# A Mamba-2 scan with a SiLU feed-forward block: products inside the chunks ordered by halves of the heads, two groups of zero products fewer, another sequence in the ramp

## The chip, the cores and the metric

The kernel runs on one core of one Trainium2 chip. The core has TensorE (PE in the profile; its weight loads are shown apart as PEld), VectorE (DVE), ScalarE (ACT), GpSimd (POOL) and SyncE (SP), which here only issues transfers. The metric is device time in microseconds, the median of several executions.

## What is computed

Two stages. The first is a state-space scan for 4 batches, 8 heads, 768 positions, head size 32 and state size 16. Cut to one chunk of positions:

```python
cum = np.cumsum(log_a, axis=-1)
L = np.exp(cum[:, :, :, None] - cum[:, :, None, :]) * causal
M = np.einsum('bhin,bhjn->bhij', Cc, Bc) * L
y_intra = np.einsum('bhij,bhjd->bhid', M, xc)
y_inter = np.einsum('bhin,bhnd->bhid', Cc, state) * np.exp(cum)[:, :, :, None]
y = y_intra + y_inter
state = decay_full[:, :, None, None] * state + sum_j(B_j x_j * decay_from_j)
```

The second takes y as 3072 tokens of 256 values: `h = y @ w_in` (256 x 2048), `g = h / (1 + exp(-h))` (SiLU), `out = g @ w_out` (2048 x 256). All inputs and outputs are float32.

## The kernel before, in words

**Units.** The 3072 positions are cut into 12 units of 256 positions; u = 0 to 11, three to a batch. A unit holds four chunks of 64 positions (chunk t = 2k + c). Two units make a pair G of 512 tokens for the feed-forward block.

**The order is written out by hand.** `SCHEDULE` (line 18) is a long text of tokens such as `M,0,1`. The table `DO` (line 857) maps a token's name to a function, the numbers are its arguments, and the loop at line 870 calls them one after the other. Each function issues a few instructions; each engine runs its own instructions strictly in the order in which the tokens come, and waits on semaphores where an operand is not ready. So the text fixes five sequences, one for each engine, and the place of two tokens of different engines relative to one another means nothing by itself. `SLOTS` (line 98) says which buffer each new tile gets, in the order in which tiles are taken.

**The tokens that matter here**, with the line that the profile shows:

- Loads: `Ln` (B or C by rows, L245), `Lt` (B or C for a transpose, L253), `Lx` (x, L260), `lw` (a block of weights, L279), `ir` (the decays for all units, L357). SP issues nearly all of them; ACT issues the first of B and C.
- `z,n` and `z,0,6` (PE, L422 and L424): products on a tile of zeros whose result nobody reads. `z,1` is one product of 128x512, `z,0,6` is six products of 64x64.
- `ab` (PE, L478) spreads the decays over partitions, `E` (DVE, L487) scans them; the result, in the tile `ab`, is the decay matrix L transposed.
- `T` (DVE, L500) or `tp`/`tq` (PE L506, ACT L515) transpose B and C; `ce` (ACT, L521) masks C by parity of the head; `C` (POOL or DVE, L526) makes cw, which is C times the decay from the chunk's start.
- `P01` (DVE, L457): prefix products of the decays, fed by `PA` (POOL, L447) and `pb` (PE, L452).
- `B` (POOL, L495) and `D` or `gd` (PE, L548): B times decay, then its products with x, the new part of the state. `S,u,t` (DVE, L590 or L592): the state after chunk t. `SM` (ACT, L600): the state masked by parity.
- `g0` (PE, L562): the products of B and C, into the PSUM tiles ga (heads 0 to 3) and gb (heads 4 to 7), each two banks. `M,u,w` (DVE, L577): half w of the heads (0: heads 0 to 3 out of ga, 1: heads 4 to 7 out of gb) times the decay matrix, written in place into `ab`.
- `Y` (PE): `products` (line 603): first 32 products inside the chunks (L613, 64 rows by 32 columns, eight at a time beside each other on the array), M times x, into ga and gb; then the products of cw and the state (L622), added to them. `X0` (ACT, L652, units 0 and 1) or `y` (ACT, L658) copy y out.
- Feed-forward, pair 0: `s` (PE, L682), `si` (ACT, SiLU, L688), `n` (PE, L748), in plain float32. The other pairs split each float32 operand into parts of fewer bits (`xh`, `x`, `h`, `l`, `e`, and for the weights `u`, `v`, `w`, `W`, `H`, `Wl`, `Wd`, `We`) and use faster products: `a`, `d` (PE, L789) and `f` (PE, L770). `u`, `v` are ACT, `w` DVE, `W` POOL (L312); `s,u,j` needs `W,j`.
- `cI` makes the identity matrix `ident`: a memset on DVE (L368), then a select on POOL (L369). `co`, `AA`, `AD` (POOL) prepare the decays of the later units and store them to DRAM.

**The ramp.** Until the first feed-forward weights are prepared and y of unit 0 exists, PE has only small work: `ab`, `pb`, `tp`, `D`, `g0`, `Y` and zero products. Then `s,0,2` is the first product of the feed-forward block, and after `Y,1` the tokens `s,0,1 s,1,2 s,1,0 ...` follow one another. From there until the end, units 2 to 11 of the scan are woven between the products of the feed-forward block.

Of the kernel before, what the change touches and what calls it, by code (L numbers as in the profile page):

```python
# [18 lines left out]
ci ia ip,0 Ln,0,0,0,1 cp cs Lt,0,1,3,1 z,1 Lt,0,1,1,1 c1 zr z,1 z,1 z,0,6 A,1 z,0,6 z,1 Lt,0,1,0,1 ab,0,0,1 Lx,0,1,0  # L19
Lt,0,1,2,1 A,0 cd ch ab,0,0,0 PA,1 cI cP E,0,0,1 Ln,0,0,1,1 c2 E,0,0,0 T,0,1 PA,0 ce,0,0 ab,0,1 B,0,0 lw,2 ce,0,1  # L20
E,0,1 pb,0 ab,1,1 B,0,1 P01,0 z,1 Lx,0,0,0 z,1 lw,1 C,0 lw,0 Ln,1,1,0,0 tp,0 D,0 u,2 tq,0 E,1,1 v,2 w,2,0 S,0,0 g0,0
S,0,1 Ln,1,0,1,0 Ln,1,1,1,0 Ln,1,0,0,0 M,0,0 Lx,1,0,0 z,0,6 M,0,1 S,0,2 v,1 w,2,1 Lx,1,1,0 u,1 w,2,2 SM,0,0 lw,3 ir,0
ab,1,0 w,1,0 S,0,3 ir,2 z,0,6 SM,0,1 u,0 Y,0 w,0,0 X0,0,0 ca X0,0,1 z,1 v,0 W,2,2,0 lw,4 ir,1 ir,3 E,1,0 lw,9 w,1,1
w,0,1 z,1 W,2,2,1 w,0,2 lw,10 s,0,2 tp,1 B,1,1 lw,8 si,0,2 tq,1 w,1,2 ce,1,1 pb,1 P01,1 B,1,0 ce,1,0 D,1 xh,0 W,0,2,0
g0,1 W,0,2,1 S,1,0 v,3 W,1,2,1 W,1,2,0 AA,0 S,1,1 M,1,0 S,1,2 SM,1,1 M,1,1 C,1 SM,1,0 AD,4 u,3 s,0,0 Ln,2,0,0,0 Y,1
x,0,0 Ln,2,1,1,0 w,3,0 AA,1 Ln,2,0,1,0 lw,11 lw,5 Ln,2,1,0,0 si,0,0 X0,1,0 La,2,0,0 Lt,3,1,0,0 X0,1,1 w,3,1 x,0,1
La,2,1,0 w,3,2 s,0,1 W,3,1,0 lw,7 u,4 H,1 w,4,0 v,9 S,1,3 si,0,1 H,2 v,4 w,4,2 w,9,2 u,10 u,9 s,1,2 si,1,2 Wd,1 s,1,0
w,4,1 u,8 v,8 co s,1,3 v,10 Lt,3,1,1,0 w,9,0 W,4,1,0 Lt,3,1,2,0 w,9,1 w,10,0 w,8,0 w,8,1 si,1,0 s,1,1 s,1,4 w,8,2
si,1,1 xh,1 si,1,3 Lx,2,0,0 u,11 W,9,1,0 w,10,2 s,0,4 v,11 AD,0 tp,2 u,5 w,11,0 Lx,2,1,0 w,5,0 Lp,2,0 w,5,1 w,11,2
si,0,4 Lt,3,0,3,0 W,8,1,0 ce,2,0 Lt,3,1,3,0 w,11,1 E,2,1 n,1 w,10,1 n,1 H,3 si,1,4 E,2,0 v,5 tq,2 AD,1 x,1,1 lw,12 n,1  # L30
# [12 lines left out]
We,1 H,13 w,15,0 La,5,0,0 S,4,3 y,4,0 La,5,1,0 AD,2 w,15,1 y,4,1 n,1 w,15,2 Wl,8 E,5,0 Wd,8 P,5 a,1,2 H,14 l,1,0
ax,1,2 a,1,1 E,5,1 Lt,5,0,3,0 e,1,0 We,9 W,15,1,0 f,1 d,1,2 ax,1,1 We,8 n,1 d,1,1 n,1 Wl,3 n,1 dg,1,2 n,1 dg,1,1 a,1,4
AD,3 f,1 H,11 h,1,1 Wl,11 T,5,1 h,1,2 We,4 ax,1,4 Vn,0 Vn,1 a,1,3 f,1 Lt,6,1,1,0 ax,1,3 Lt,5,0,1,0 ce,5,1 d,1,4 f,2
e,1,1 We,3 Lt,6,1,2,0 We,5 Wl,10 d,1,3 f,1 Ln,5,0,1,0 ce,5,0 f,1 B,5 f,1 Lt,6,1,0,0 l,1,2 f,1 e,1,2 dg,1,4 f,1 l,1,1
Wd,10 dg,1,3 Wl,12 f,1 Lt,5,0,2,0 f,1 Lx,5,0,0 gd,5 T,5,0 g0,5 f,3 We,10 xh,4 f,1 b,5,0 Lt,6,1,3,0 Wd,11 f,1 C,5 M,5,1
f,1 b,5,1 h,1,3 a,1,5 f,3 S,5,0 f,1 T,6,1 ax,1,5 f,1 h,1,4 f,1 S,5,1 d,1,5 f,1 S,5,2 SM,5,1 f,2 M,5,0 dg,1,5 Wd,13
Wl,13 l,1,3 f,2 SM,5,0 Lx,6,1,0 x,4,0 Lt,6,0,2,0 Lt,7,1,2,0 We,12 Lt,6,0,0,0 ce,6,0 La,6,1,0 Ln,6,0,1,0 x,4,1 f,2 Y,5
l,1,4 H,15 La,6,0,0 Lt,6,0,1,0 ce,6,1 e,1,3 E,6,0 f,1 Lt,7,1,3,0 f,1 y,5,1 Lt,7,1,0,0 f,1 a,1,7 Wd,15 f,1 We,11 ax,1,7  # L50
f,2 Lt,6,0,3,0 Lt,7,1,1,0 f,1 E,6,1 f,2 d,1,7 f,2 T,6,0 f,1 Ln,6,0,0,0 B,6 Lx,6,0,0 f,1 Lp,6,0 f,1 y,5,0 f,1 xh,5 f,1
dg,1,7 g0,6 x,5,0 Lt,7,0,3,0 gd,6 Lt,7,0,0,0 e,1,4 f,1 Wl,15 f,3 Ln,7,0,1,0 Lt,7,0,2,0 f,1 P,6 M,6,1 b,6,0 Wl,14 M,6,0
La,7,0,0 S,6,0 a,2,1 Wd,14 b,6,1 a,1,6 S,6,1 x,5,1 f,1 ax,2,1 h,1,5 f,1 Lt,7,0,1,0 S,6,2 l,1,5 ax,1,6 d,2,1 f,1 SM,6,0
dg,2,1 d,1,6 f,1 C,6 f,2 e,1,5 We,13 dg,1,6 o,0,1,2 S,6,3 T,7,1 f,1 We,15 SM,6,1 f,1 h,1,6 f,1 Y,6 T,7,0 y,6,1 y,6,0
# [851 lines left out]
```

## Time and profile before

| | |
|---|---|
| Median of 3 runs | 325.53 us (325.52 to 325.64) |
| Profiled execution: its time / its span | 325.91 us / 324.2 us |
| Mean granted clock of TensorE | 0.999 |
| DVE, ACT, POOL busy in the span | 239.1, 210.6, 71.4 us |
| PE: L770, 480 products | 112.1 us (hp) and 31.3 us (o_ps) |
| PE: L789, 504 products | 62.3 (ga), 61.6 (gb), 4.3 (hp) and 3.0 us (gb, first weights) |
| PE: L748 / L682 | 30.3 us / 22.1 us |
| PE: L613, 768 products' records | 7.2 + 7.2 + 1.7 + 1.4 us |
| PE: L422 (8) and L424 (24), on zeros | 3.3 us and 1.6 us |
| Transfers | 30.64 MB, 80312 of 95794 packets under 512 B |
| DMA share, 14.4 to 22.4 us / 22.4 to 319.7 us | 0.97 / 0.41 |

How to read it: "busy" counts an engine from an instruction's start to its end, overlaps once. The ends of matmuls are modelled and matmuls overlap in the array, so that a busy PE may still be waiting; the prediction therefore also uses times from start to start. A float32 product stands in the trace as two records (two passes), each with its weight load. The chain of waits goes back from the last instruction to whatever released it. A pause marked "issue" is one that no other engine ended, as far as the profile shows.

### The profile page before, as it was taken

How to read it: one execution, taken by the hardware profiler on the slowest of the kernel's cores; microseconds unless marked ns; L12 is line 12 of the kernel's file. 1: busy time of each engine (PE TensorE's matmuls, PEld its weight loads, DVE VectorE, ACT ScalarE, POOL GpSimd, SP SyncE). 2: the span in 40 equal slices, each digit the busy share in tenths (PEclk: the TensorE clock that was granted, in tenths of full speed). 3: DMA queues.
4: the chain of work that ended last, by engine and by line, in shares of the span. 5: the costliest groups of instructions: out<-in, count | busy, mean ns of one | idle time of the engine just before them, and what ended most of it. 6: DMA issues, size and time to landing. Idle time of an engine off the chain costs nothing.

```text
span 324.2 us, 7544 instructions
## 1 busy us (share of the span) xinstructions
PE 318.6 (98%) x3060; PEld 243.2 (75%) x3060; DVE 239.1 (74%) x335; ACT 210.6 (65%) x326; POOL 71.4 (22%) x88
## 2 busy tenths in 40 slices
PE   8999999999999999999999999999999999999995
PEld 4678655665677777877878877878887888888883
DVE  6998998987896779974896858985397644365753
ACT  2889866889687755975655767636766554865442
POOL 6476563555624040300300000010010000000000
PEclk9999999999999999999999999999999999999999
DMA  7999894987578564730422544324001100003102
GB/s 154 191 321 241 226 184 128 214 170 158 103 130 156 105 133 111 143 45 2 87 59 36 114 86 70 63 46 91 2 0 30 30 0 0 2 8 57 19 0 65
DMA packets 95794, 30.64 MB, mean 95 GB/s; under 512 B 80312, under 2 KB 86968, under 8 KB 95760
## 3 DMA queue, kind: packets, MB, share of 16 engines
q1 hardware_dynamic: 90592, 25.38, 35.7%
q0 software_dynamic: 2480, 4.39, 7.7%
q10 hardware_dynamic: 2688, 0.39, 0.7%
q8 instruction: 24, 0.39, 0.5%
q14 instruction: 10, 0.08, 0.1%
HBM read 22.61 MB, written 3.34 MB: 80 GB/s over the span
## 4 chain that ended last, share of the span: by engine, by line
PE 93%; DVE 2%; ACT 1%; DMA 1%; ACTq 1%; issue 0%; DVEq 0%
PE hp L770 29%; PE gb L789 18%; PE ga L789 17%; PE hp L748 9%; PE hp L682 6%; PE o_ps L770 6%; PE ga L622 2%; PE ga L562 2%; PE ga L613 2%; DMA s2k<-in_C_dram 1%; PE ga L548 1%; PE gb L613 1%; PE hp L789 1%; DVE ab L487 1%; ACTq L253 0%
## 5 line engine op out<-in xcount | busy, mean ns | idle before, releaser
L770 PE MATMUL hp<-r4k,s2k 128*128 128x512 f32 x400 | 112.1, 392 | 0.0
L770 PEld LDWEIGHTS hp<-r4k,s2k 128*128 128x128 f32 x400 | 74.7, 188 | 16.0 <-issue 0.3
L642 DVE SCALAR_TENSOR_TENSOR r4k<-r4k,r4k 128x1024 fp32r<-128x1024 f32 (+1 forms) x42 | 50.6, 1204 | 30.6 <-ACT r4k L832 15.7
L639 DVE SCALAR_TENSOR_TENSOR r4k<-r4k,r4k 128x1024 fp32r<-128x1024 f32 (+1 forms) x42 | 51.1, 1223 | 18.4 <-PE hp L770 8.2
L789 PE MATMUL ga<-raw,s2k 128*128 128x512 f32 x240 | 62.3, 395 | 0.0
L789 PE MATMUL gb<-raw,s2k 128*128 128x512 f32 x240 | 61.6, 392 | 0.0
L789 PEld LDWEIGHTS ga<-raw,s2k 128*128 128x128 f32 x240 | 44.9, 188 | 11.0 <-issue 1.0
L789 PEld LDWEIGHTS gb<-raw,s2k 128*128 128x128 f32 x240 | 44.9, 188 | 10.2 <-ACT gb L800 0.6
L832 ACT ACTIVATE r4k<-r4k 128x1024 fp32r<-128x1024 f32 x40 | 42.0, 1056 | 1.4 <-PE hp L770 1.2
L800 ACT ACTIVATE ga<-ga 128x1024 f32<-128x1024 f32 x20 | 20.2, 1009 | 26.3 <-PE ga L789 26.3
L495 POOL TENSOR_TENSOR BT<-bn,ab 128x256 f32<-128x256 f32 x10 | 10.0, 997 | 100.9 <-DVE ab L487 47.7
L800 ACT ACTIVATE gb<-gb 128x1024 f32<-128x1024 f32 x21 | 21.2, 1010 | 16.8 <-PE gb L789 16.7
L770 PE MATMUL o_ps<-r4k,s2k 128*128 128x512 f32 x80 | 31.3, 397 | 0.0
L748 PE MATMUL hp<-r4k,s2k 128*128 128x512 f32 x64 | 30.3, 600 | 0.0
L810 ACT ACTIVATE r4k<-ga 128x1024 f32<-128x1024 f32 x20 | 20.5, 1025 | 14.6 <-PE ga L789 12.7
L312 POOL TENSOR_TENSOR s2k<-s2k,s2k 128x512 uint32<-128x512 uint32 (+1 forms) x19 | 26.3, 1392 | 13.9 <-DVE s2k L301 7.8
L810 ACT ACTIVATE r4k<-gb 128x1024 f32<-128x1024 f32 x21 | 21.5, 1022 | 6.1 <-PE gb L789 4.5
L487 DVE TENSOR_TENSOR_SCAN ab<-ab,diag 128x512 f32<-128x512 f32 x20 | 24.0, 1214 | 0.4 <-DMA ab<-az 0.4
L682 PE MATMUL hp<-r4k,s2k 128*128 128x256 f32 x96 | 22.1, 383 | 0.0
L682 PEld LDWEIGHTS hp<-r4k,s2k 128*128 128x128 f32 x96 | 17.8, 190 | 4.1 <-issue 1.3
L748 PEld LDWEIGHTS hp<-r4k,s2k 128*128 128x128 f32 x64 | 11.6, 189 | 9.7 <-issue 8.6
L770 PEld LDWEIGHTS o_ps<-r4k,s2k 128*128 128x128 f32 x80 | 15.0, 188 | 3.4 <-issue 0.2
(127 smaller groups left out, 402.4 us busy)
## 6 DMA issues: line engine op xcount, KB each, us to landing
ab<-az SPq DMA_DIRECT2D x20, 256.0 KB
raw<-in_moe_w_in_dram SPq DMA_DIRECT2D x8, 512.0 KB
raw<-in_moe_w_out_dram SPq DMA_DIRECT2D x8, 512.0 KB
s2k<-s2k POOLq DMA_DIRECT2D x16, 256.0 KB, 4.2
out_dram<-r4k SPq DMA_DIRECT2D x44, 64.0 KB
xt<-in_x_dram SPq DMA_DIRECT2D x20, 128.0 KB
pz<-ac SPq DMA_DIRECT2D x10, 130.0 KB
bn<-in_B_dram SPq DMA_DIRECT2D x20, 64.0 KB
```

Source lines behind the costliest of these rows:

```text
L312: nc.gpsimd.tensor_tensor(out=dst[:, :, fs].bitcast(U32), in0=u[:, :, fs], in1=v[:, :, fs], op=ALU.add)
L487: nc.vector.tensor_tensor_scan(out=o, data0=src, data1=heads(diag, half).rearrange("p h t -> p (h t)"), initial=0.0, op0=ALU.mult, op1=ALU ...
L495: nc.gpsimd.tensor_tensor(out=BT[u][:, ks], in0=bn[u][:, ks], in1=E[u][:, ks, :, Q - 1:Q].to_broadcast([128, n, H, N]), op=ALU.mult)
L639: nc.vector.scalar_tensor_tensor(out=l, in0=f32(h), scalar=BACK, in1=y, op0=ALU.mult, op1=ALU.add)
L642: nc.vector.scalar_tensor_tensor(out=d, in0=f32(h), scalar=-(BACK + 1.0), in1=y, op0=ALU.mult, op1=ALU.subtract)
L682: nc.tensor.matmul(out=hp[:, i], lhsT=WT[j][:, kc, 128 * i:128 * i + 128], rhs=XM[:, 2 * kc:2 * kc + 2, u], start=(kc == 0), stop=(kc == K ...
L748: nc.tensor.matmul(out=NP["o"][m], lhsT=WT[8 + f // 2][:, f % 2, 128 * m:128 * m + 128], rhs=GT[0, f // 2][:, f % 2], start=(f == 0), stop ...
L770: nc.tensor.matmul(out=ACC[P, 2 * (p == "d") + m], lhsT=WK[8 + f // 2, p][:, f % 2, 128 * m:128 * m + 128], rhs=rhs, start=(f == 0 and p ! ...
L789: nc.tensor.matmul(out=o, lhsT=WK[j, q][:, kc, 128 * i:128 * i + 128], rhs=xs[:, 2 * kc:2 * kc + 2], start=(start and q == "h" and kc == 0 ...
L800: nc.scalar.activation(t, t, AF.Copy, scale=1.0 + Z)
L810: nc.scalar.activation(g, t, AF.Silu, scale=BACK)
L832: nc.scalar.activation(t, GT[G, i], AF.Copy, scale=-LESS * Z)
```

## The change

In `products` two loops change places, so that heads 0 to 3 get their products for both k before heads 4 to 7:

```diff
-        for k in range(2):
-            cols = slice(c0 + 64 * k, c0 + 64 * k + 64)
-            for w in range(2):
+        for w in range(2):
+            for k in range(2):
+                cols = slice(c0 + 64 * k, c0 + 64 * k + 64)
                 for c in range(2):
                     for q in range(4):
                         h = 4 * w + q
```

The text `SCHEDULE` is changed from its first line to the token ahead of `S,6,0`; all behind it is the same. Two tokens `z,0,6` are gone. All other tokens are the same in kind and number, except that some `n,1` and `f,1` are joined (`n,2`, `f,2`), with as many products in all. The buffers in `SLOTS` are given out anew to fit. The first lines:

```diff
-ci ia ip,0 Ln,0,0,0,1 cp cs Lt,0,1,3,1 z,1 Lt,0,1,1,1 c1 zr z,1 z,1 z,0,6 A,1 z,0,6 z,1 Lt,0,1,0,1 ab,0,0,1 Lx,0,1,0
-Lt,0,1,2,1 A,0 cd ch ab,0,0,0 PA,1 cI cP E,0,0,1 Ln,0,0,1,1 c2 E,0,0,0 T,0,1 PA,0 ce,0,0 ab,0,1 B,0,0 lw,2 ce,0,1
-E,0,1 pb,0 ab,1,1 B,0,1 P01,0 z,1 Lx,0,0,0 z,1 lw,1 C,0 lw,0 Ln,1,1,0,0 tp,0 D,0 u,2 tq,0 E,1,1 v,2 w,2,0 S,0,0 g0,0
-S,0,1 Ln,1,0,1,0 Ln,1,1,1,0 Ln,1,0,0,0 M,0,0 Lx,1,0,0 z,0,6 M,0,1 S,0,2 v,1 w,2,1 Lx,1,1,0 u,1 w,2,2 SM,0,0 lw,3 ir,0
-ab,1,0 w,1,0 S,0,3 ir,2 z,0,6 SM,0,1 u,0 Y,0 w,0,0 X0,0,0 ca X0,0,1 z,1 v,0 W,2,2,0 lw,4 ir,1 ir,3 E,1,0 lw,9 w,1,1
+ci ia ip,0 Ln,0,0,0,1 Lt,0,1,3,1 cs Lt,0,1,1,1 z,1 zr z,1 z,1 z,0,6 Lt,0,1,0,1 c1 z,0,6 ch cp z,1 A,1 Lt,0,1,2,1 A,0
+cd Lx,0,1,0 Ln,0,0,1,1 c2 ab,0,0,1 cP E,0,0,1 ab,0,0,0 PA,0 E,0,0,0 T,0,1 ab,0,1 cI E,0,1 pb,0 ce,0,0 B,0,0 P01,0
+B,0,1 C,0 lw,2 ce,0,1 Lx,0,0,0 lw,1 lw,0 u,2 ab,1,1 z,1 z,1 tp,0 D,0 tq,0 E,1,1 g0,0 v,2 S,0,0 Ln,1,0,1,0 PA,1 ca
+w,2,0 S,0,1 M,0,1 Ln,1,0,0,0 u,1 M,0,0 v,1 Ln,1,1,0,0 z,1 S,0,2 w,2,1 z,1 Ln,1,1,1,0 Lx,1,0,0 w,2,2 SM,0,1 ab,1,0
+Lx,1,1,0 lw,3 W,2,2,0 SM,0,0 w,1,0 ir,2 ir,0 E,1,0 Y,0 ir,3 u,0 X0,0,0 X0,0,1 v,0 S,0,3 W,2,2,1 lw,4 ir,1 B,1,0 w,0,0
```

Sorted by engine, the two sequences of the ramp are (- before, + after):

```
PE   - z,1 z,1 z,1 z,0,6 z,0,6 z,1 ab ab ab pb,0 ab,1,1 z,1 z,1 tp,0 D,0 g0,0 z,0,6 ab,1,0 z,0,6 Y,0 z,1 z,1 s,0,2 tp,1 pb,1 D,1 g0,1 s,0,0 Y,1 s,0,1
PE   + z,1 z,1 z,1 z,0,6 z,0,6 z,1 ab ab ab pb,0 ab,1,1 z,1 z,1 tp,0 D,0 g0,0 z,1 z,1 ab,1,0 Y,0 s,0,2 tp,1 pb,1 D,1 g0,1 s,0,0 Y,1 s,0,1
DVE  - E,0,0,0 T,0,1 E,0,1 P01,0 E,1,1 w,2,0 S,0,0 S,0,1 M,0,0 M,0,1 S,0,2 w,2,1 w,2,2 w,1,0 S,0,3 w,0,0 E,1,0 w,1,1 w,0,1 w,0,2 w,1,2 P01,1 S,1,0 S,1,1 M,1,0 S,1,2 M,1,1 C,1 x,0,0
DVE  + E,0,0,0 T,0,1 cI E,0,1 P01,0 E,1,1 S,0,0 w,2,0 S,0,1 M,0,1 M,0,0 S,0,2 w,2,1 w,2,2 w,1,0 E,1,0 S,0,3 w,0,0 w,0,1 w,1,2 w,0,2 w,1,1 P01,1 S,1,0 S,1,1 S,1,2 M,1,0 M,1,1 C,1 x,0,0
ACT  - ce,0 u,2 tq,0 v,2 v,1 u,1 SM,0,0 SM,0,1 u,0 X0,0,0 X0,0,1 v,0 si,0,2 tq,1 ce,1,1 ce,1,0 xh,0 v,3 SM,1,1 SM,1,0 u,3 si,0,0 X0,1,0 X0,1,1 u,4
ACT  + ce,0 u,2 tq,0 v,2 u,1 v,1 SM,0,1 SM,0,0 u,0 X0,0,0 X0,0,1 v,0 si,0,2 ce,1,1 ce,1,0 tq,1 xh,0 SM,1,1 SM,1,0 u,3 H,2 v,3 si,0,0 u,4 X0,1,0 X0,1,1
POOL - cs c1 ch PA,1 cI c2 PA,0 B,0,0 B,0,1 C,0 ca W,2 W,2 B,1,1 B,1,0 W,0 W,0 W,1 W,1 AA,0 AD,4 AA,1 W,3 co W,4 W,9 AD,0 W,8
POOL + cs c1 ch c2 PA,0 cI B,0,0 B,0,1 C,0 PA,1 ca W,2 W,2 B,1,0 B,1,1 W,0 W,0 W,1 W,1 AA,0 co AA,1 AD,4 AD,0 W,3 W,4 W,8 W,9
SP   - Lx lw,2 Lx lw,1 lw,0 Ln,1,1,0 Ln,1,0,1 Ln,1,1,1 Ln,1,0,0 Lx Lx lw,3 ir,0 ir,2 lw,4 ir,1 ir,3 lw,9 lw,10 lw,8
SP   + Lx lw,2 Lx lw,1 lw,0 Ln,1,0,1 Ln,1,0,0 Ln,1,1,0 Ln,1,1,1 Lx Lx lw,3 ir,2 ir,0 ir,3 lw,4 ir,1 lw,9 lw,10 lw,8
```

Behind this and up to `S,6,0` neighbours change places in the same manner: loads of units 2 to 7, steps of the weight preparation, single `n` and `f` products, and the order of the two `SM` or two `M` of some units. In the changed kernel `M,u,1` stands ahead of `M,u,0` in units 0, 4, 5, 6, 8 and 9.

## The prediction

> **What bounds the kernel now.** I read the page first, then the waits of PE, then the chain of waits over the first 24 us, then the timelines of single engines where that chain leaves PE.
>
> ```profile
> PE 318.6 (98%) x3060; PEld 243.2 (75%) x3060; DVE 239.1 (74%) x335; ACT 210.6 (65%) x326; POOL 71.4 (22%) x88
> ...
> q8 instruction: 24, 0.39, 0.5%
> ...
> PE 93%; DVE 2%; ACT 1%; DMA 1%; ACTq 1%; issue 0%; DVEq 0%
> ```
>
> PE holds 93% of the chain, and the kernel's own PE work is the same before and after. Next, all that PE waited for (total, times, longest):
>
> ```profile
> PE o_ps L422 <- DVE s2k L362: 1.3, 1, 1.3
> PE ga L722 <- DVE r4k L712: 0.5, 1, 0.5
> PE ga L562 <- ACT ce L521: 0.3, 1, 0.3
> PE ga L622 <- ACT sm L600: 0.2, 1, 0.2
> ```
>
> The first is the start, the second the tail at 320 us; neither is touched. Ends of matmuls are modelled, so I also took start-to-start times of PE from the trace. From 22.34 us, where s,0,1 begins, to 319 us I find no pause beyond the steps that recur with each change of operation. After 22.34 us nothing can be won unless PE work gets cheaper, and the ramp is worth what it brings 22.34 us forward. This is the chain up to there (start, length, what):
>
> ```profile
> 2.88 3.84 DMA s2k<-in_C_dram
> ...
> 6.84 0.64 DVE ct L500
> 7.48 1.01 DVE ab L487
> ...
> 10.19 0.32 DVE s2k L294
> 10.51 0.14 DVE st L590
> ...
> 12.46 0.65 ACT sm L600 x2
> ...
> 15.09 1.28 ACT L688
> ...
> 17.26 0.74 ACT ce L521 x2
> ...
> 18.74 1.92 PE hp L682 x8
> ...
> 21.43 0.11 issue
> 21.55 0.24 PE gb L613
> ```
>
> C lands, DVE works through unit 0 without a rest, ACT makes sm, PE ends Y,0, ACT copies it (X0), loads its Silu table, evaluates si,0,2 and makes ce of unit 1; then PE has s,0,0 and Y,1 and never rests again. The last two lines are a pause inside Y,1 that no engine ends. The weight loads show it:
>
> ```profile
> 21.05 0.22 PEld L613 LDWEIGHTS gb<-ab,s2k 64*32 64x32 f32 x14
> 21.55 0.10 PEld L613 LDWEIGHTS gb<-ab,s2k 64*32 64x32 f32 x1 [0.27 <-issue]
> ```
>
> Between the last two products of one group PE got no instruction: 0.328 us start to start where this place takes 0.017 in the other units, so 0.31 us are lost. I read it as a late block of PE's instructions: queue q8 moved 24 packets for 6120 PE instructions, one per 255; the pause stands at about the 706th recorded PE instruction, the block before began near the 450th (17.38 us, in D,1), and the DMA share from 17 to 22 us is 0.93. This is my reading, not something the trace says.
>
> **The change, part by part.**
>
> **1. DVE's order in unit 0.** Before, w,2,0 stands ahead of S,0,0, and S,0,1 must wait for S,0,0's result:
>
> ```profile
> 10.43 0.22 DVE L590 COPY st<-hp 128x64 f32<-128x64 f32 x1
> 10.76 0.28 DVE L592 SCALAR_TENSOR_TENSOR st<-st,s2k,hp 128x64 f32<-128x64 f32 x1
> ```
>
> S,0,0 to S,0,1 takes 0.33 us from start to start, though the 0.22 us copy lets an independent instruction follow after some 0.14. With w,2,0 between them (0.32 us from its start to the next one's) the wait is filled: 0.14 + 0.32 in place of 0.32 + 0.33, a gain of **0.19 us** on the path. Against it, ident's memset (0.17 us) moves from 3.94 us, where DVE was waiting, to behind T,0,1 on the path. It costs its start-to-start time: at least 0.09 (DVE instructions overlap by some 0.08), at most 0.17; I take **0.09**. Net **-0.10 us**, between -0.19 and 0. It carries through: SM, X0, W,2, the table load and ce follow in the same sequence, and the last pieces before g0,1 (si,0,2, then tq,1 and the two ce) only change places. M,0,1 ahead of M,0,0 is the same 0.6 + 0.6 us.
>
> **2. Ident's second half on POOL** now waits for that memset with B,0,0, B,0,1 and C,0 queued behind it. It runs from about 7.6 to 7.9 us; B,0,0 slides from 6.56 to 7.9, B,0,1, which waits for E,0,1, only from 8.57 to 8.66. D,0 and g0,0 move by 0.1 and M,0 still finds them done (10.25 against 10.86). Cost nothing; DVE's scan covers it. PA,1 behind C,0 is wanted at 16.7 us. PA,0 comes earlier, but pb,0 follows ab,0,1 with no gap now: no gain.
>
> **3. Two groups z,0,6 fewer; two z,1 earlier.** The removed groups run at 10.18 and 11.54, 0.38 us each, while PE waits for M,0 and then for sm (13.25). The z,1 pair at 13.76 ends before X0 and W,2 let s,0,2 begin. The path gains nothing by their going: **0**. What they may hold up, the clock, is a rival below.
>
> **4. Halves outermost.** The first product waits for M,u,0 as before; the products of heads 4 to 7 need M,u,1 eight products later than they did. This can only loosen a wait, and outside unit 0 PE finds M done in all units. In unit 0 the new DVE order makes M,0,0 the later half, so that all 32 products begin at about 12.2 and take the 0.64 us of an undisturbed unit: 12.8, under the 13.15 at which sm lets L622 go. If sm's cover were gone it would cost up to 0.3. On PE itself the order touches twelve groups of 0.64 us. The first 32 records of a unit (two a product) take 0.24 us from start to start, the rest 0.40; if the new order brought all to the first pace, -0.16 each, -1.9 us in all; all to the second, +1.9. But the slow pace does not follow the tile: in unit 0 PE resumes at the 17th record, after M,0,1, and again 32 records run at about 7 ns before it slows, now at the step to gb, while the step from gb to ga costs 5 ns there. I take **0**, by that row.
>
> **5. The pause in Y,1.** Twelve zero products fewer are 24 PE instructions, all ahead of it. If it is a block's end, it moves 24 instructions on, into the L622 products. Block asked for: at 17.38 + 0.09 - 0.10, as before; there: at about 21.5, as before. PE gets to that point at 21.24 - 0.10 + 0.15 (step to L622) + 0.1 = 21.38 and loses about 0.14 instead of 0.31: **-0.17 us**. Bounds: -0.31 (gone), and, if the block comes 0.5 us later behind the reordered loads, +0.5.
>
> **6. The rest (SP's loads, weight preparation to 110 us).** SP issues the same loads, neighbours exchanged; the lw stay in place until lw,11 and lw,5. The tightest weight is WT3: co and AD,0 now stand ahead of W,3. From AA,0 at 21.33: 0.9 with its memset, 0.4 co, 0.9 AA,1, 0.8 AD,4, 0.8 AD,0, 1.3 W,3, gaps included about 26.8; s,1,3 wants it at 27.53 - 0.3. Cover 0.4 us. X0,1 is done by about 23.5 with v,3 and u,4 ahead of it, s,1,2 starts at 23.8. W,8 gets earlier. Cost **0**, with up to +0.5 if one cover fails. The n and f groups that move are as many as before and PE is full either way.
>
> **Sum:** -0.10 - 0.17 = **-0.27 us**. The profiled execution took 325.91 (span 324.2, 1.7 outside it); it becomes 325.64, span 323.9. The median of the runs shown is 0.38 lower: 325.53 - 0.27 = 325.26, given as **325.25 us**.
>
> **Rivals.**
>
> *A. The clock falls (slower).* The zero products also keep PE active. Rows of the zero products at the start and later:
>
> ```profile
> 1.26 1.46 PE L422 MATMUL o_ps<-s2k 128*128 128x512 bf16 x3 [1.26 <-DVE s2k L362]
> 13.76 0.60 PE L422 MATMUL o_ps<-s2k 128*128 128x512 bf16 x2
> ```
>
> Early ones start 0.4 us apart, later ones 0.22: PE begins at half pace and is faster by 7 us. The change takes the last filler between ab,1,0 (11.6) and s,0,2 (14.3), where only 1.2 us of small products remain. If PE fell back there for as long as it took at the start (1.3 to about 6 us), s,0,2, the transposes and small products on the path would double: some +2.2 us, 327.5. It decides when PE's work in that stretch is too little. For it: the fillers there now make up 1.0 of the 2.7 us. Against it: the other pauses are 0.6 us at most, and from 16.2 to 18.7 PE already does 1.8 us of work in 2.5 without a fall. Chance 0.07.
>
> The Trainium skill says on this ("TensorE: Matmul & The Clock Gate", Part 1) that the array runs at half rate until it has been busy for a window of about 3.4 us and falls back after an idle one. The two paces in the rows agree with its two rates; by that rule pauses of 0.6 us change nothing, and the sum stays.
>
> *B. The pause stays, or another comes with the new sequence.* Only term 1: 325.43. With a longer pause or a failed cover, +0.5 over that, 325.9; beyond 326.2 when both come. Chance 0.20 within 0.2%, 0.07 beyond.
>
> *C. The order of the products speeds PE up.* -0.06 a unit gives 324.5; for it speaks that the rest of a unit is slower than its start, against it unit 0 as above. Chance 0.10.
>
> *D. The change does nothing*, the ramp being held by C's landing and the table load: 325.5. It lies in the range. Chance 0.12; the forecast has 0.44.
>
> **How the numbers follow.** 0.2% is 0.65 us, about what a measurement of this kernel can tell from no change. Faster by more: C, 0.10. Slower by more: A and the end of B, 0.14. Same: 0.76. The range leaves out A, the far end of B and the greater part of C, 0.2 in all: 324.8 to 326.2.
>
> **What would show it.** M,0 starting near 10.86, sm at 12.36, s,0,0 at 18.6, s,0,1 near 22.07 in place of 22.34, and from there the same PE stretch. Term 5 is wrong if the pause stays in the last L613 products or vanishes; term 4 if the twelve groups do not keep 0.64 us; A would show in L682's spacing (0.216 us per record now) before 20 us. A new entry among PE's waits after 22 us makes the forecast wrong.

## The result and the profile after

The changed kernel takes **327.23 us** (median of 20 executions, 325.76 to 330.28) against 325.71 for the kernel before on the same chip (325.49 to 326.87): a ratio of 1.0062, 95% interval 1.0039 to 1.0086. It is slower, by about 0.6%; the forecast was 325.25, the same within 0.2%. The profiled execution took 328.11 us with a span of 326.4. (One correction to the text above: the two weight matrices come as float64, 512 KB a load, and are turned to float32 by `u`, `v`, `w` and `W`; the other inputs are float32. No number of the prediction hangs on it.) Ratios here and below leave out executions more than 1.5% longer than the fastest of their kernel; the ranges and medians keep them.

Page of the changed kernel, part 1 and part 4 (busy time, then the chain that ended last, by engine):

```profile
PE 317.6 (97%) x3047; PEld 242.8 (74%) x3048; DVE 238.4 (73%) x335; ACT 210.4 (64%) x326; POOL 68.8 (21%) x88
...
q8 instruction: 24, 0.39, 0.5%
...
PE 93%; DVE 2%; ACT 1%; DMA 1%; issue 1%; ACTq 1%; DVEq 0%
```

PE does 1.0 us less than before and ends later; "issue" has risen from 0% to 1%. What PE waited for (total, times, longest):

```profile
PE ga L622 <- issue: 2.3, 1, 2.3
PE o_ps L422 <- DVE s2k L362: 1.3, 1, 1.3
PE hp L682 <- POOL s2k L312: 0.6, 1, 0.6
PE ga L613 <- DVE ab L577: 0.5, 1, 0.5
PE ga L722 <- DVE r4k L712: 0.5, 1, 0.5
```

The first line is new and holds the loss. The third and fourth are places where zero products used to stand: PE waits there as it had to before, only visibly. PE's weight loads in Y,1:

```profile
20.58 0.29 PEld L613 LDWEIGHTS ga<-ab,s2k 64*32 64x32 f32 x32 [0.33 <-DVE ab L577]
20.77 0.50 PEld L613 LDWEIGHTS gb<-ab,s2k 64*32 64x32 f32 x32
...
21.48 0.19 PEld L622 LDWEIGHTS ga<-cw,sm 32*64 32x64 f32 x2
24.02 0.13 PEld L622 LDWEIGHTS ga<-cw,sm 32*64 32x64 f32 x1 [2.35 <-issue]
```

The pause that stood between the last two L613 products is now among the L622 products, as term 5 placed it, but it is 2.49 us from start to start instead of 0.33. s,0,1 begins at 24.53 us (22.34 before). From there to the last product of L770 it is 296.94 us, before 296.92: the whole loss of the profiled execution lies in this pause.

### The profile page after: what moved, and what is told of

Same layout as the page of the kernel before. It is cut to its first block, busy times and chain, and to the rows that moved or that the text cites. A ratio compares the mean times of both kernels' runs of the same rounds, so it can differ in the third digit from the quotient of the medians.

```text
span 326.4 us, 7522 instructions
## 1 busy us (share of the span) xinstructions
PE 317.6 (97%) x3047; PEld 242.8 (74%) x3048; DVE 238.4 (73%) x335; ACT 210.4 (64%) x326; POOL 68.8 (21%) x88
## 4 chain that ended last, share of the span: by engine, by line
PE 93%; DVE 2%; ACT 1%; DMA 1%; issue 1%; ACTq 1%; DVEq 0%
PE hp L770 28%; PE gb L789 18%; PE ga L789 17%; PE hp L748 9%; PE hp L682 6%; PE o_ps L770 6%; PE ga L622 2%; PE ga L562 2%; PE gb L613 1%; PE ga L613 1%; DMA s2k<-in_C_dram 1%; PE ga L548 1%; PE hp L789 1%; DVE ab L487 1%; ACTq L253 0%
## 5 line engine op out<-in xcount | busy, mean ns | idle before, releaser
L770 PE MATMUL hp<-r4k,s2k 128*128 128x512 f32 x400 | 111.9, 393 | 0.0
L770 PEld LDWEIGHTS hp<-r4k,s2k 128*128 128x128 f32 x400 | 74.6, 188 | 16.1 <-issue 0.3
L642 DVE SCALAR_TENSOR_TENSOR r4k<-r4k,r4k 128x1024 fp32r<-128x1024 f32 (+1 forms) x42 | 50.8, 1210 | 30.9 <-ACT r4k L832 15.7
L639 DVE SCALAR_TENSOR_TENSOR r4k<-r4k,r4k 128x1024 fp32r<-128x1024 f32 (+1 forms) x42 | 52.2, 1248 | 18.2 <-PE hp L770 8.0
L770 PE MATMUL o_ps<-r4k,s2k 128*128 128x512 f32 x80 | 31.1, 395 | 0.0
L312 POOL TENSOR_TENSOR s2k<-s2k,s2k 128x512 uint32<-128x512 uint32 (+1 forms) x19 | 24.6, 1308 | 18.5 <-DVE s2k L301 11.4
L495 POOL TENSOR_TENSOR BT<-bn,ab 128x256 f32<-128x256 f32 x10 | 8.2, 821 | 95.4 <-DVE ab L487 67.3
L810 ACT ACTIVATE r4k<-gb 128x1024 f32<-128x1024 f32 x21 | 21.5, 1022 | 6.5 <-PE gb L789 4.8
L487 DVE TENSOR_TENSOR_SCAN ab<-ab,diag 128x512 f32<-128x512 f32 x20 | 24.9, 1263 | 0.3 <-DMA ab<-az 0.3
L682 PE MATMUL hp<-r4k,s2k 128*128 128x256 f32 x96 | 22.1, 383 | 0.6 <-POOL s2k L312 0.6
L682 PEld LDWEIGHTS hp<-r4k,s2k 128*128 128x128 f32 x96 | 17.9, 190 | 4.2 <-issue 1.1
L748 PEld LDWEIGHTS hp<-r4k,s2k 128*128 128x128 f32 x64 | 11.6, 189 | 8.4 <-issue 7.1
L331 POOL DMA_DIRECT2D s2k<-s2k x16 | 14.5, 1024 | 15.4 <-ACT s2k L327 6.8
```

Source lines behind the costliest of these rows:

```text
L312: nc.gpsimd.tensor_tensor(out=dst[:, :, fs].bitcast(U32), in0=u[:, :, fs], in1=v[:, :, fs], op=ALU.add)
L331: nc.gpsimd.dma_start(out=f32(WK[n, p]).rearrange("p k f -> p (k f)"), in_=other.rearrange("p k f -> p (k f)"), accum_op=ALU.add)
L487: nc.vector.tensor_tensor_scan(out=o, data0=src, data1=heads(diag, half).rearrange("p h t -> p (h t)"), initial=0.0, op0=ALU.mult, op1=ALU ...
L639: nc.vector.scalar_tensor_tensor(out=l, in0=f32(h), scalar=BACK, in1=y, op0=ALU.mult, op1=ALU.add)
L642: nc.vector.scalar_tensor_tensor(out=d, in0=f32(h), scalar=-(BACK + 1.0), in1=y, op0=ALU.mult, op1=ALU.subtract)
L682: nc.tensor.matmul(out=hp[:, i], lhsT=WT[j][:, kc, 128 * i:128 * i + 128], rhs=XM[:, 2 * kc:2 * kc + 2, u], start=(kc == 0), stop=(kc == K ...
```

## The experiments

The trace's transfer records show 24 packets of 16 KB on queue q8, 256 instructions of 64 bytes each. Counted with its own semaphore instructions, PE's stream stops in Y,1 at instruction 704 in every kernel that pauses there, give or take one. The next such edge ahead is 448, in D,1. That the count, and not the kind of the product, sets the place I took as good evidence for a block's end, and asked what makes the block late. The theory at the start was **a late block, placed by the number of PE instructions and made late by SP's loads**; the rivals were the exchanged loops themselves, the zero products as a load on PE's clock, and SP's order alone. The theory changed twice on the way.

All kernels were run with five rounds beside the kernel before. The diffs give tokens of `SCHEDULE`, cut at "..."; where one engine's order is the matter, its tokens alone.

**e1: the exchanged loops alone**, in the kernel before.

> The kernel before, with the two loops of the products exchanged and nothing else. Theory of the late block (PE stands in Y,1 until its next block of 256 instructions has landed behind the loads of the weights): the loops change neither the number of PE instructions nor the loads, so 325.7 us like before, each L613 group 0.64 us, the pause in Y,1 0.3 us. Rival, the order of the products slows PE: 327 us or more, spread over the twelve L613 groups.

```diff
-        for k in range(2):
-            for w in range(2):
+        for w in range(2):
+            for k in range(2):
```

Measured 325.78 (325.45 to 326.47), ratio 0.9998 [0.9988, 1.0007]; each L613 group keeps its 0.64 us. The loops are not the cause.

**e2: the two groups of zeros out**, in the kernel before.

> The kernel before without its two groups of six zero products (24 PE instructions), all else as before. Late block: the block's edge moves 24 instructions on, into the L622 products of Y,1; with the loads of before it lands near 21.5 us, so a pause of 0 to 0.5 us there and 325.4 to 325.9 us. Rival, the zero products hold the clock or the pace of PE up: 327 us or more, and a lower clock or slower spacing between 11 and 20 us.

```diff
-M,0,0 Lx,1,0,0 z,0,6 M,0,1      -S,0,3 ir,2 z,0,6 SM,0,1
+M,0,0 Lx,1,0,0 M,0,1            +S,0,3 ir,2 SM,0,1
```

326.64 (325.81 to 330.09), ratio 1.0039 [1.0015, 1.0063]. This alone brings more than half of the loss, and the pause (0.9 us, where 0 to 0.5 was expected) sits in L622, at the place of the changed kernel:

```profile
21.69 0.19 PEld L622 LDWEIGHTS ga<-cw,sm 32*64 32x64 f32 x3
22.71 0.13 PEld L622 LDWEIGHTS ga<-cw,sm 32*64 32x64 f32 x1 [0.83 <-issue]
```

**e3: the two groups back in the changed kernel**, on both sides of `ab,1,0`.

> The changed kernel with two groups of six zero products put back around ab,1,0. Late block: the edge goes back into the last L613 products of Y,1 (at 21.2 us), the loads are those of the changed kernel, so the block still lands near 24 us at worst: pause of 0.3 to 2.8 us there and 326 to 330 us, as scattered as the changed kernel. Rival, the zero products make the difference: 325.2 to 325.7 us, no pause.

```diff
-SM,0,1 ab,1,0 Lx,1,1,0
+SM,0,1 z,0,6 ab,1,0 z,0,6 Lx,1,1,0
```

327.85 (325.68 to 332.37), ratio 1.0045 [1.0020, 1.0071]; the pause is 1.57 us and back in the last L613 products, at 23.31 us. So the number of instructions sets the place, and putting them back does not cure the lateness: there is a second cause.

**e4 and e5: the edge moved out of Y,1**, with 86 and 68 PE instructions more in the changed kernel.

> The changed kernel with small zero products in place of some large ones and 18 more behind ab,1,0: 86 PE instructions more ahead of Y,1, where PE waits for DVE and ACT anyway. Late block: the block that was awaited in Y,1 is now asked for at 13.4 us, when the queues carry little, and wanted at 20.9 us; the pause of 2.4 us is gone, the ramp ends near 22.0 us, 325.1 us, with little scatter. Rival, the new sequence itself (loads, weight preparation) delays PE: still 326.5 us or more.

> The changed kernel with 68 PE instructions more ahead of Y,1 (zero products: z,0,12 for z,1 z,1 twice, z,0,14 behind ab,1,0), the shift for which every 256 PE instructions take at least 5.6 us. Late block, with 4.2 to 6.6 us from an edge to the arrival of the block asked for there: no pause over 1 us anywhere, s,0,1 near 22.1 us, 325.2 us, between 324.9 and 325.8. Rival, the new sequence of the ramp delays PE by itself: 326.5 us or more without such a pause.

```diff
-ab,1,1 z,1 z,1 tp,0    -z,1 S,0,2 w,2,1 z,1 Ln,1,1,1,0    -ab,1,0 Lx,1,1,0
+ab,1,1 z,0,12 tp,0     +S,0,2 w,2,1 z,0,12 Ln,1,1,1,0     +ab,1,0 z,0,14 Lx,1,1,0
```

(e5; e4 has `z,0,18` in the last place and one `z,1` of the start as `z,0,6`.) e4: 326.79, ratio 1.0030 [1.0015, 1.0044]; e5: 327.34, ratio 1.0041 [1.0020, 1.0062]. In both the pause in Y,1 is gone (s,0,1 at 22.22 and 22.45 us), and one as long stands three edges on, at 57.3 and 57.9 us, at instruction 1472 or one behind it (e4, then e5):

```profile
PE ga L562 <- issue: 2.2, 1, 2.2
```

```profile
PE hp L682 <- issue: 2.2, 1, 2.2
```

My hope that a shift alone makes a faster kernel fell; that the pauses go with the count of instructions is shown.

**e6 and e7: the kernel before with 44 PE instructions more, and with the two groups moved ahead of `tp,0`.**

> The kernel before with 44 PE instructions more ahead of Y,1, in the same manner, again the best shift. Late block: the pause of 0.3 us and more in Y,1 goes, 325.3 us, and the runs scatter less than those of before. If the loops or the zero products counted instead: as before, 325.8 us, or slower.

> The kernel before with its two groups of six zero products moved ahead of tp,0 (8.3 us), so that as many PE instructions as before stand ahead of Y,1 and none of them are near 10 and 11.5 us. Late block: as before, 325.8 us, the pause in the last L613 products of Y,1. Rival, the zero products are needed at 10 to 12 us to keep PE's pace: 326.6 us or more, like the kernel without them.

```diff
-P01,0 z,1 Lx,0,0,0 z,1 lw,1    -ir,2 z,0,6    -X0,0,1 z,1 v,0    -w,0,1 z,1 W,2
+P01,0 z,0,12 Lx,0,0,0 lw,1     +ir,2 z,0,8    +X0,0,1 v,0        +w,0,1 z,0,12 W,2
...
-P01,0 z,1     -Lx,1,0,0 z,0,6 M,0,1    -ir,2 z,0,6 SM,0,1
+P01,0 z,0,6 z,0,6 z,1    +Lx,1,0,0 M,0,1    +ir,2 SM,0,1
```

e6: 325.86, ratio 0.9999 [0.9990, 1.0008], where 325.3 was expected; nothing is read from its trace. e7: 326.15 (325.72 to 326.67), ratio 1.0013 [1.0005, 1.0022], without a pause in Y,1 (0.3 us was expected) and without e2's long executions, though the stretch from 11.6 to 14.3 us has as few zeros as in e2. With e2 and e3 this speaks against the clock (rival A): it is the count ahead of the edge that matters, not PE's work in that stretch. Why e7 is still 0.1% slower than the kernel before was not followed up.

**e8: SP's loads alone**, the first 28 in the changed kernel's order, in the kernel before.

> The kernel before with the first 28 loads on SP in the order of the changed kernel, all other engines as before. If the order of the loads makes the block late: the pause stays in the last L613 products of Y,1 and grows to 1 to 2.5 us, 326.5 us or more with scatter. If it does not: 325.8 us.

```diff
-Ln,1,1,0,0 Ln,1,0,1,0 Ln,1,1,1,0 Ln,1,0,0,0 ... ir,0 ir,2 lw,4 ir,1 ir,3 ... Ln,2,0,0,0 Ln,2,1,1,0 Ln,2,0,1,0 lw,11 lw,5
+Ln,1,0,1,0 Ln,1,0,0,0 Ln,1,1,0,0 Ln,1,1,1,0 ... ir,2 ir,0 ir,3 lw,4 ir,1 ... Ln,2,0,1,0 Ln,2,0,0,0 lw,11 lw,5 Ln,2,1,1,0
```

325.43 (324.96 to 325.98), ratio 0.9990 [0.9981, 0.9998]; no pause in Y,1. The theory that the new order of loads brings the late block fell here.

**e9, e10, e12: the loads as a burden.** e9 issues lw,9, lw,10 and lw,8 behind two loads of unit 2 in the changed kernel; e10 and e12 add 512 KB of loads to the kernel before, behind lw,10 and ahead of lw,9.

> The changed kernel with three loads of expert weights (lw,9, lw,10, lw,8; 512 KB each) issued behind two loads of B for unit 2 instead of ahead of them, so that SP issues them at about 17.5 to 22 us instead of 16.7 to 18.9 and up to 1.5 MB less stand in the DMA queues when PE asks for the block of instructions that it needs in Y,1. Theory 1 (the block waits behind the weight loads that are already in the queues): its 16 KB packet starts at about 18 to 19 us instead of 21.18, the pause of 2.49 us in the L622 products shrinks to 0 to 0.5 us, s,0,1 starts near 22.1 instead of 24.53, and the median falls from 327.2 to 325.2 to 325.8 if the weights that come later are not missed, with a spread under 1.5 us. Theory 2 (the block waits for something else, such as the order on the engines, or the number of PE instructions alone): the pause stays at 1.5 to 3 us and the median at 326.8 or above.

> The kernel before with three loads more on SP between lw,10 and lw,8 (512 KB in all, into tiles that nothing reads before they are written again; the result is the same): the suspected load on the DMA queues made larger. Theory 1 (queues full of weights hold up the block of PE instructions): the packet that starts at 19.20 us before starts 1 to 1.6 us later, the pause in Y,1 grows from 0.31 to 1.2 to 1.9 us, s,0,1 starts at 23.2 to 23.9 instead of 22.34, the median rises from 325.8 to 326.6 to 327.5, and single executions reach 329. Theory 2 (the queues do not matter, the position of the block's edge and the sequence do): the pause stays between 0 and 0.9 us as in the kernels with the loops exchanged or with after's loads alone, and the median within 325.4 to 326.2.

> The kernel before with the three spare loads of e10 (512 KB in all) ahead of lw,9 instead of behind lw,10, so that they stand in SP's queues when PE asks for the block at about 17.5 us. If the block waits behind the loads already queued: its packet starts at 20 to 21 us instead of 19.2, the pause in Y,1 grows from 0.31 to 1.2 to 2 us and the median goes to 326.5 to 327.5. If not: the pause stays under 0.9 us and the median within 325.4 to 326.2.

```diff
-tp,1 lw,9 lw,10 pb,1 ... lw,8 D,1 ... AA,0 lw,11
+tp,1 pb,1 ... D,1 ... AA,0 lw,9 lw,10 lw,8 lw,11
...
-lw,10 s,0,2                      -E,1,0 lw,9
+lw,10 lz,0 lz,1 lz,2 s,0,2       +E,1,0 lz,0 lz,1 lz,2 lw,9
```

e9: the pause falls from 2.49 to 1.03 us, but PE now waits 0.8 us in D,1 for x, and at 31 us (0.86 us from start to start) for a Silu result that stands behind a late weight on ACT; the time stays at 327.16, ratio 1.0045 [1.0029, 1.0060]. e10: 325.99, ratio 1.0014 [1.0004, 1.0024]; e12: 327.00, ratio 1.0035 [1.0021, 1.0049], but **not by the late block**: it has no pause in Y,1, and PE waits later for a Silu result whose weight came late.

```profile
PE hp L690 <- ACT r4k L696: 0.7, 1, 0.7
```

(Its lines stand 8 higher: L690 is L682.) Going by the time alone, e12 would have seemed to bear out the expectation. In e10 and e12 the block's packet starts at 18.11 and 17.69 us, ahead of all that was added: the loads of e12 were issued from 17.48 us on, so PE seems to have asked for the block before that, not at 17.4 to 17.9 as I had thought from the products.

**e11: loads and loops together**, the edits of e8 and e1 in the kernel before.

> The kernel before with the loads of SP in the changed kernel's order and with the halves of the heads outermost, which each alone measured 325.43 and 325.78. If the parts add up as their own results say: 325.3 to 325.6, no pause over 0.6 us in Y,1, twelve groups of L613 at 0.64 us each; a version that is as fast as the best so far. If the two parts together, without the fewer zero products, already bring the late block: 326.5 or above and a pause of 1 us or more.

325.64 (325.21 to 325.95), ratio 0.9996 [0.9988, 1.0005].

**e13, e14, e15: the other engines' orders.** e13 is e3 with the two `z,1` back behind Y,0, so that PE has its old sequence. e14 is e11 with DVE's new order, e15 is e14 with ACT's and POOL's new order.

> The changed kernel with PE's sequence in the ramp as it was before (both groups z,0,6 and the two z,1 at their old places), only the halves and the orders of the other engines and of SP remain. If the places and the number of the zero products bring the late block: packet of the block before 19.5 us, pause under 0.9 us, median 325.4 to 326.2. If the order of DVE, ACT and POOL brings it: packet after 20 us, pause 1.3 us or more, median 326.8 to 328, executions up to 330.

> The kernel with the changed kernel's loads and halves (e11, 325.64) and, added, DVE's order of the ramp as in the changed kernel (w,2,0 behind S,0,0, ident's memset behind T,0,1, M,0,1 first, E,1,0 ahead of S,0,3). If DVE's order brings the late block: 326.8 to 328 with a pause of 1.3 us or more in Y,1. If not: 325.3 to 326.1, pause under 0.9 us; by term 1 of the prediction the ramp would be 0.1 us shorter at most, which this measurement can hardly show.

> The kernel of e14 with ACT's and POOL's order of the ramp as in the changed kernel too, so that against the changed kernel only PE's zero products (two groups z,0,6 more, two z,1 later) and the order after 22 us differ. If the order of the other engines brings the late block: packet after 20 us, 326.8 to 328. If the zero products do: packet before 19.5 us, median 325.3 to 326.1, spread under 1.5 us. Exactly one of this run and e13 should show the late block if one cause is enough.

```diff
-Ln,1,1,0,0 z,1 S,0,2 w,2,1 z,1 Ln,1,1,1,0 ... w,0,0 s,0,2
+Ln,1,1,0,0 S,0,2 w,2,1 Ln,1,1,1,0 ... w,0,0 z,1 z,1 s,0,2
...
-cI cP ... T,0,1 E,0,1 ... w,2,0 S,0,0 S,0,1 M,0,0 M,0,1 ... S,0,3 w,0,0 E,1,0
+cP ... T,0,1 cI E,0,1 ... S,0,0 w,2,0 S,0,1 M,0,1 M,0,0 ... E,1,0 S,0,3 w,0,0
...
-v,1 u,1 SM,0,0 SM,0,1 ... tq,1 ce,1,1 ce,1,0    -PA,1 cI c2 PA,0 ... B,1,1 B,1,0
+u,1 v,1 SM,0,1 SM,0,0 ... ce,1,1 ce,1,0 tq,1    +c2 PA,0 cI ... PA,1 ... B,1,0 B,1,1
```

e13: 326.06 (325.24 to 332.25), ratio 1.0020 [0.9999, 1.0041], with a pause of 1.16 us. e14: **325.51** (325.18 to 325.97), ratio 0.9991 [0.9981, 1.0000], s,0,1 at 21.99 us. e15: 327.22 (325.57 to 330.18), ratio 1.0056 [1.0027, 1.0084]. So ACT's or POOL's order holds the second cause. It shows in the instructions of L548, that is D,1, which the trace lists with the waits that PE's sequencer ran as instructions of their own. e14, then the changed kernel:

```profile
L548 PEldq EVENT_SEMAPHORE  x1: 51/51/51, 16.0 to 16.0; - x1
```

```profile
L548 PEldq EVENT_SEMAPHORE  x3: 51/51/51, 15.1 to 17.3; - x3
```

One wait at 16.0 us, 1.3 us ahead of D,1's products: PE's stream runs ahead of its products. With POOL's B,1,0 ahead of B,1,1, one wait for POOL no longer covers both halves of D,1: the second half needs B,1,1 and its own part of x, and gets a wait instruction for that x. It is passed at 17.34 us, 0.02 us after D,1's first weight load, though B,1,1 had ended at 16.16 and that part of x had landed at 16.52 us: neither result was late, the stream came to this wait only as D,1 began.

**e16, e17, e18: that swap by itself.** e16: the changed kernel with POOL's B,1,1 first again. e17: the same and the zeros back (e3 with the swap). e18: e14 with B,1,0 first.

> The changed kernel with B,1,1 ahead of B,1,0 on POOL, as before; the zeros stay out. Theory (PE asks for its next block when its instruction stream, which runs ahead of its products, gets to the 448th instruction; a wait inside D,1 holds that up, and so do 24 instructions fewer ahead of it): the wait inside D,1 is gone, but the request still lies some 40 instructions behind the start of D,1, as in e2, which measured 326.64: here 326.2 to 327.2, block packet at 19.5 to 21, pause 0.5 to 1.6 us. Rival (only POOL's order counts): 325.3 to 325.9, no pause over 0.3 us.

> The changed kernel with B,1,1 ahead of B,1,0 and the two groups z,0,6 back on both sides of ab,1,0 (e3 with the swap). Theory: the request comes before PE's wait ahead of D,1 ends, at about 16.3 us, the block's packet starts by 19.3 us, the pause in Y,1 is 0 to 0.4 us, s,0,1 starts at 22.0 to 22.4, median 325.2 to 325.9 and no execution over 327 (e3: 327.85, up to 332.4). Rival (the order of ACT, or of the rest of POOL, brings the late block): 326.8 or above with a pause of 1 us or more.

> The kernel of e14 (325.51, on time) with B,1,0 ahead of B,1,1 on POOL and nothing else. Theory: PE has a wait of its own inside D,1 at the 441st instruction, asks for its block only at about 17.4 us, behind more weight loads; packet after 19.4 us, pause 0.4 to 1.6 us, median 326.2 to 327.4 with executions over 328. Rival: as e14, 325.3 to 325.8.

```diff
-tp,1 B,1,1 lw,8 si,0,2 ... P01,1 B,1,0 ce,1,0 D,1
+tp,1 B,1,0 lw,8 si,0,2 ... P01,1 B,1,1 ce,1,0 D,1
```

(e18; e16 and e17 are the same the other way about.) **e17: 326.11 (325.79 to 326.30), ratio 1.0003 [0.9991, 1.0016]**, packet at 17.64 us, no pause in Y,1. e18: 326.92 (325.63 to 332.00), ratio 1.0029 [1.0006, 1.0053], and its traces differ from e14's by one wait in D,1 and a pause in Y,1:

```profile
L548 PEldq EVENT_SEMAPHORE  x2: 51/51/51, 15.9 to 17.5; - x2
```

```profile
20.92 0.48 PEld L613 LDWEIGHTS gb<-ab,s2k 64*32 64x32 f32 x30
21.98 0.13 PEld L613 LDWEIGHTS gb<-ab,s2k 64*32 64x32 f32 x2 [0.57 <-issue]
```

e16: 326.85 (325.87 to 331.45), ratio 1.0041 [1.0016, 1.0067]; its profiled execution, its fastest, loses only about 0.26 us in Y,1 (1.67 us from the first L613 product to s,0,1, in e14 1.41). The two edits together account for the loss: either alone brings about half to three quarters of it (e2 and e16 the zeros, e3 and e18 the swap), so that the two do not add up, and with both undone nothing is left (e17).

The kernels side by side. "Last wait" is the last wait of L548 in the trace (where there is one in D,1's middle, that one; else the one ahead of D,1 for the first part of x), "issued" the 512 KB weight loads that SP had begun to issue by then, "packet" the start of the block's transfer, and "begun" the 2 KB packets of weights begun by the packet's start, divided by the 256 of a load (both counted in the transfer records); the pause is from start to start in Y,1.

| kernel | last wait us | issued | begun | packet us | pause us | ratio |
|---|---|---|---|---|---|---|
| e8 | 15.73 | 4 | 4.0 | 18.07 | 0 | 0.9990 |
| e14 | 16.05 | 4 | 4.0 | 18.05 | 0 | 0.9991 |
| e17 | 15.62 | 4 | 4.0 | 17.64 | 0 | 1.0003 |
| e10 | 15.99 | 4 | 4.0 | 18.11 | 0 | 1.0014 |
| e12 | 16.07 | 4 | 4.0 | 17.69 | 0 | 1.0035 |
| e11 | 15.68 | 4 | 4.2 | 18.16 | 0 | 0.9996 |
| before | 15.80 | 5 | 4.8 | 19.20 | 0.33 | 1 |
| e7 | 16.04 | 5 | 5.0 | 18.87 | 0 | 1.0013 |
| e1 | 17.00 | 5 | 4.5 | 19.89 | 0.54 | 0.9998 |
| e13 | 17.37 | 5 | 4.3 | 19.63 | 1.16 | 1.0020 |
| e15 | 17.57 | 5 | 4.9 | 19.89 | 0.79 | 1.0056 |
| e9 | 17.94 | 5 | 4.9 | 20.44 | 1.03 | 1.0045 |
| e18 | 17.49 | 6 | 4.8 | 19.70 | 0.63 | 1.0029 |
| e3 | 17.88 | 6 | 5.1 | 20.87 | 1.57 | 1.0045 |
| after | 17.34 | 7 | 6.2 | 21.18 | 2.49 | 1.0062 |

Read in this way the rows agree, as if the block were asked for when the stream gets past D,1's last wait: its packet starts when at most 1.2 of the weight loads issued by then are still to begin. It is a matter of tenths, and both counts grow with time anyway, so that this is a reading and not a proof. SP's timeline in e14 (lw,4, then lw,9 to lw,8), with the last wait at 16.05 us, so that the block goes ahead of lw,4:

```profile
16.52 0.39 SPq L279 DMA_DIRECT2D raw<-in_moe_w_in_dram  x1
...
17.43 2.15 SPq L279 DMA_DIRECT2D raw<-in_moe_w_out_dram  x3
```

And in the changed kernel, where it comes at 17.34 us, with lw,4, lw,9 and lw,10 (17.09 us, within the x3) in front:

```profile
15.76 0.39 SPq L279 DMA_DIRECT2D raw<-in_moe_w_in_dram  x1
16.19 0.43 SPq L357 DMA_DIRECT2D s2k<-in_a_dram  x1
16.66 2.19 SPq L279 DMA_DIRECT2D raw<-in_moe_w_out_dram  x3
```

PE goes on 1.3 to 1.5 us after the end of the packet wherever it pauses in Y,1 (22.62 to 24.02 here, 20.29 to 21.55 before). e2 and e16 stand outside the table: they have no wait within D,1 (last waits 16.04 and 15.66 us), but the 448th instruction lies 39 and 38 behind D,1's first instruction instead of 14 or 15 (in the changed kernel and e9 it lies 38 behind as well), and begun is 5.3 and 4.7 (packets at 20.48 and 19.41 us): as if asked for when D,1 ran, at 17.5 us.

What stays open is how each edit delays the request. Each kernel's own list of PE instructions gives the order that the trace, sorted by time, does not. In the changed kernel and e9 the wait in D,1's middle stands 6 instructions ahead of the 448th, so the stream got there only after 17.34 and 17.94 us. But in e3, e13, e15 and e18 it stands 18 behind it: there it can't hold back a request sent at the 448th itself. That the swap makes the block late is shown (e3 against e17, e14 against e18); that it does so through this wait is not. Nor is it shown why 38 or 39 is too far (e2, e16): set beside that list, a wait is passed at most 42 instructions ahead of what PE has begun in any trace, and those in D,1's middle at most 26 ahead. That the packet waits for the loads in front is read off the counts; loads added surely ahead of the request were not tried (those of e12 seem to have come after it). And a profile shows one execution of a pause that differs from one to the next.

## Why the prediction failed, point by point

**The step that failed is 5, its line "Block asked for: at 17.38 + 0.09 - 0.10, as before; there: at about 21.5, as before".** The edge moved by 24 instructions as said, and to the L622 products as said. But the time of the request is not that of the product at the edge ahead. Before, PE's stream was past its only wait ahead of D,1, for x, at 15.8 us, and so could ask while PE stood ahead of D,1:

```profile
L548 PEldq EVENT_SEMAPHORE  x1: 51/51/51, 15.8 to 15.8; - x1
```

In the changed kernel it passes the last wait ahead of the edge about 1.5 us later (17.34 us), behind two more loads of weights, and the packet starts at 21.18 instead of 19.20 us. The pause went from 0.33 to 2.49 us where -0.17 was forecast, and my upper bound of +0.5 was priced on reordered loads, which e8 shows to do no harm. The working did not weigh the two edits that bring the late request: the zeros (24 instructions that, as argued above, kept the edge within reach of the stream while PE stood ahead of D,1) under step 3, and POOL's B,1,0 and B,1,1 under step 6. Of the signs named ahead, the last one showed, a new entry among PE's waits (L622, 2.3 us); the signs given for term 5, that the pause stays in L613 or vanishes, left out that it could grow.

**Step 1** (-0.10): the swap gave 0.21 us, as estimated (0.19), but the memset of `ident` cost 0.19, more than its own 0.17 and twice the 0.09 taken (it seems to lose the overlap of the two instructions that it separates). M,0 starts at 10.94 us instead of 10.96: -0.02.

```profile
6.84 0.64 DVE L500 STREAM_TRANSPOSE ct<-s2k 128x256 f32<-128x256 f32 x1 [0.36 <-DMA s2k<-in_C_dram]
7.43 0.17 DVE L368 MEMSET ident<- 128x128 f32 x1
7.52 1.16 DVE L487 TENSOR_TENSOR_SCAN ab<-hp,diag 128x512 f32<-128x512 f32 x1
```

The scan begins at 7.52 us; before it was 7.33.

**Step 2** (0): held; D,0 and g0,0 are done ahead of M,0. **Step 3** (0): held for the path, PE's own waits there cost nothing; its price lies in the count of instructions. **Step 4** (0): held; e1, and 0.64 us a group in all units. **Step 6** (0): no weight is late and nothing is lost behind s,0,1; what was missed is the order of B,1,0 and B,1,1, with the wait inside D,1.

**The rivals.** A (clock, 327.5 us) comes nearest to the measured time by accident: in the profiled execution the clock is at full rate from 5.8 us on, and e7 has as few zeros there at 0.1%. B had the right kind, a longer pause, but was priced at 0.5 us. C is excluded by e1. D fell.

## What to carry to other kernels

Count the instructions of an engine that runs many short ones: where 256 of them take only a few microseconds, the next block comes beside a burst of weight loads, and an edit that costs nothing in busy time can cost 2 us by when that block is asked for. Look also at the waits of such a group: here, letting the part that is needed first be made last, so that one wait ahead of the group covers both, kept the block in time (e14 and e17 against e18 and e3). For a pause marked "issue" the range is to be as wide as the transfers that can come in front of the block, not as the pause that was seen.

## What the runs showed of the hardware

A block of 16 KB is fetched during the run, on a queue (q8) that the page counts with the data on the core's 16 DMA engines, and PE stood still at a block's edge for up to 2.6 us (e5). The Trainium skill ("Runtime: NRT & Kernel Launch", section "Instruction fetch mechanics") says that the instruction memory is refilled in blocks of 16 KiB or 256 instructions while the engine works, and that crossing to the next is mostly hidden. The trace agrees on the blocks (24 packets of 16 KB for some 6120 instructions); on the hiding the measurement decides: here it cost 2.49 us in the changed kernel.

The spread seems to come from the same place: e14 and e17 stay within 0.8 and 0.5 us, while e3, e15 and e18, late kernels all, reach 330 to 332 us (e9, late as well, stays within 1.5 us). In the 20 executions of the changed kernel the seven longest spans (327.5 to 328.5 us) have a mean clock of 0.994 or 0.995, the others 0.997 to 1.0; 0.005 of 326 us is 1.6 us. I read it as the clock falling after the longest pauses, but none of them was profiled. The clock records of the profiled executions, e6 aside, show full rate for 317.44 or 320.85 us, steps of 3.41 us, and a fall only at the end. The Trainium skill ("TensorE: Matmul & The Clock Gate", Part 1) gives an idle window of about 3.4 us after which the array goes at half rate. An estimate from that page, one such window at half rate, lowers the mean by 3.4 x 0.5 / 326 = 0.005, the step that is seen; no trace here shows it in the middle of a run.

The fastest versions are e8 and e14, 0.1% under the kernel before at the most likely, less than the 0.2% that the prediction took as what a measurement of this kernel can tell.
